# When a unit's copies are issued, and new orders for the first six tiles, in a convolution fused with a two-matmul layer

## Chip, core and metric

One core of one Trainium2 chip runs the whole kernel. The metric is the device time of one execution in microseconds (us); the time of a kernel is the median of its runs.

## What is computed

```python
def _attn_ref(x, weight):                 # x: 8 x 4096 x 192, weight: 8 heads x 7 taps
    w = weight - np.max(weight, axis=-1, keepdims=True)
    w = np.exp(w)
    w = w / (np.sum(w, axis=-1, keepdims=True) + 1e-09)
    ...
    x_unf = x_pad[:, idx, :].reshape(B, S, K, H, group)      # causal: a position and the six before it
    out = np.einsum('hk,bskhg->bshg', w, x_unf)

def _moe_ref(x, w_in, w_out):             # w_in: 192 x 2048, w_out: 2048 x 192
    h = x @ w_in
    g = h * np.cos(h)
    return (g @ w_out).astype(np.float32)
```

The output of the first function, as 32768 rows of 192, is the input of the second. The inputs and the output are float32; the kernel multiplies in bfloat16.

## The kernel before

**Tiles and units.** The 32768 rows are worked in 64 tiles of 512 rows; two tiles make a unit of 1024 rows. A tile t belongs to the unit u = t // 2; an even tile is the first of its unit, an odd one the second.

**A tile.** TensorE (PE) makes eight products h0 to h7 with w_in (`mm1`, L524; six matmuls each) into a ring of three PSUM buffers. For each, ScalarE (ACT) takes the cosine as a shifted sine (s0 to s7, L531) and VectorE (DVE) multiplies it with h to g (L535). The second matmul (`mm2_step`, L573) adds up g times w_out in 64 steps per tile, two matmuls each. It runs behind the first: steps of one tile are spread over the orders of that tile and the next. Its first 32 steps and its last 32 write the same banks with other row halves, so between them the code sets a marker on SP's queue (`Turn`, L203): SP passes it when step 32 is done, and PE waits for it before step 33. The place is called q in the orders. The end of a tile's 64 steps is p; then ACT and DVE copy the result out (P, Q, L592), and O stores it (L595).

**The convolution.** The input of a unit is loaded (L), cast to bfloat16 by GpSimd (POOL) (K, L218), and part of it goes through matmuls with a band matrix on PE (c1, c2: L284, eight matmuls each, with another of the markers on SP's queue between c1 and c2) and ACT's copies (ec1, ec2) into `ct_buf`; SP transposes that by DMA into `ro` (X and x, L326). The other part is transposed raw (T, L353) and its seven taps are multiplied and added up on ACT (a0 to a2, L377) and POOL (R, L386; S, L393 to L396, the last of which writes `ro`). At last SP issues four copies from `ro` into `cT`, the matmuls' input for that unit (U, `spread_raw`, L408 and L409). `cT` has two buffers.

The first three units (0 to 2) go another way: their convolution is done on PE alone (`conv_first`, `conv_rest` r, `conv_part` d1, c1, d2, c2; L236, L486), ACT or DVE copies it out (er, ed, ec, L493, L246; with a small e on ACT, with a capital E on DVE), POOL doubles it (D) and mends its edges (Y), SP transposes it into cT (X, L334).

**What sets the order.** Nothing is scheduled by a planner: the program is written out in strings, one for PE with SP's and POOL's work in it, one for ACT and DVE. `PE_ORDER` and `ACT_ORDER` hold the even and the odd tile of the steady part, `PE_FIRST` and `ACT_FIRST` the first tiles, whose last two entries for ACT are `ACT_ORDER`. "m7" is seven steps of the second matmul, "h3" a product of the first, "w5" five matmuls on zeros into a bank that nobody reads (`keep_warm`, L143), and a letter with "+2" means that work for the unit u + 2. Each engine runs its own instructions in the order in which the strings name them, and waits where data is missing. SP's instructions (all loads, stores, transposes, copies and the markers) form one queue.

**The start.** `LOADS` orders the loads on SP: b is the second half of unit 0, l, r and e are the halves and edge rows of unit 1, and 0 to 3 are quarters of w_out, each by two DMAs (L128); those behind the bar are issued when the first convolution is copied out (L459). POOL casts each quarter (W0 to W3, L124). Step k of the first 32 in tile 0 needs quarter k // 8.

Of the kernel before, what the change touches and what calls it, by code (L numbers as in the profile page):

```python
# [16 lines left out]
def kernel(  # L17
# [9 lines left out]
    B, S, D = x.shape  # L27
    H, K = weight.shape
# [3 lines left out]
    T = 512  # L32
    NT = NTOK // T
    NB = T // 128
    U = 1024
    NU = NTOK // U
    UB = U // 128
# [5 lines left out]
    R = G // NC  # L43
# [9 lines left out]
    PA = 3  # L53
# [66 lines left out]
    wo_src = moe_w_out.rearrange("(i j p) d -> p j i d", i=2, p=128)  # L120

    def cast_wo(q):
        have.add(("wo", q))
        nc.gpsimd.tensor_copy(out=wo[:, q * QP : (q + 1) * QP], in_=wo_f[:, q * QP : (q + 1) * QP])  # L124

# [11 lines left out]
    zero = consts.tile([128, T], BF16)  # L137
# [74 lines left out]
    bf, xk = {}, {}  # L212

    def cast_unit(u, n0=0, n1=UB + 1, copy=nc.gpsimd.tensor_copy):
        if u >= FIRST_RAW:
            xk[u] = xk_pool.tile([128, NC * (UB + 1), 64], BF16, name="xk")
            for n0, n1 in ((NPB, UB + 1), (0, NPB)):
                copy(out=xk[u][:, NC * n0 : NC * n1].rearrange("p (k n) m -> p k n m", k=NC),  # L218
                     in_=x_tiles[u][:, n0:n1].rearrange("p n (m k) -> p k n m", k=NC))
            if u % UPS == 0:  # L220
                nc.gpsimd.memset(xk[u][0 : 128 - OP, 0 : NC * NPB : NPB], 0.0)
            return
        if n0 == 0:
            bf[u] = xb0 if u == 0 else xbf_pool.tile([128, UB + 1, D], BF16, name="x_bf")
        o = 1 if u == 0 else 0
        copy(out=bf[u][:, n0 + o : n1 + o, :].rearrange("p n (h k r) -> p (n h) k r", k=NC, r=R),  # L226
             in_=x_tiles[u][:, n0:n1, :].rearrange("p n (h r k) -> p (n h) k r", k=NC, r=R))

    ct_tiles = {}
    have = {("whole", 0, 0)}  # L230
# [24 lines left out]
    def conv_part(u, c, banks, whole=False):  # L255


        ps = banks()
        nb = UB + 1
        for i in range(4):  # L260
            conv_mm(u, c, ps, i, slice(0, 128), 0, nb, start=i % 2 == 0, stop=i % 2 == 1)
        if u == 1 and c == 0:
            spread_taps(ps[1][:, nb * 2 * G : nb * 2 * G + K])
        yield
        yield
        if u not in ct_tiles:
            ct_tiles[u] = ct_pool.tile([128, UB + 1, NC, 2, 64], BF16, name="ct")
        for b in range(2):
            conv_out(u, c, ps, 0, 0, nb, copies[by[0]], banks=(b,))
            if b and u == 1 and c == 0:  # L270
                nc.scalar.copy(tap, ps[1][:, nb * 2 * G : nb * 2 * G + K])
            if b:
                have.add(("conv", u, c))
            yield

    def conv_unit(u, banks):


        ps = banks()
        sides = [slice(0, 64), slice(64, 128)]  # L280

        def mm(h, side):
            first, last = h % 4 == 0 and h // 4 == side, h % 4 == 3 and h // 4 != side
            return nc.tensor.matmul(  # L284
                out=ps[h // 4][:, 0 : NPB * 4 * G].rearrange("p (m i r) -> p i m r", m=NC * NPB, i=4)[:, h % 4],
                lhsT=band[sides[side], h, 128 - OP : 256 - OP], rhs=xk[u][sides[side], 0 : NC * NPB, R * h : R * (h + 1)],
                start=first, stop=last, skip_group_check=True)

        for h in range(4):
            ms = mm(h, 0), mm(h + 4, 1)  # L290
        turn = Turn()
        turn.mark(*ms)
        yield
        for h in range(4):
            ms = mm(h + 4, 0), mm(h, 1)
            if h == 0:
                turn.wait(*ms)
        yield
        both = ps[0].tensor, ps[0].offset, [ps[0].ap[0][0], OP]
        for n0, n1 in ((1, NPB), (0, 1)):  # L300
            to = ct_bufs[u % 2][0:OP, 2 * NC * min(n0, 1) : 2 * NC * (min(n0, 1) + 1)]
            to = to.rearrange("p (k n) (b w) -> p b k n w", k=NC, b=2)[:, :, :, 0 : n1 - n0]
            nc.scalar.copy(to, bass.AP(both[0], both[1] + 4 * R * n0, [both[2], [T, 2], [NPB * 4 * R, NC], [4 * R, n1 - n0], [1, 4 * R]]))  # L303
            if n0 == 0:
                have.update((("conv", u, 0), ("conv", u, 1)))
            yield
# [32 lines left out]
    tap = consts.tile([128, K], FP32)  # L339
# [42 lines left out]
    def tap_raw(u):  # L382

        p = raw_prod
        for j in range(NG):
            nc.gpsimd.tensor_scalar(out=p[:, j], in0=tap_window(u, PA + j), scalar1=tap[:, PA + j : PA + j + 1],  # L386
                                    scalar2=1.0, op0=ALU.mult, op1=ALU.mult)

    def sum_raw(u):

        assert {("tap", u, j, PARTS[k].start) for j in range(PA) for k in "lr"} <= have
        a, p, add = pa.pop(u), raw_prod, nc.gpsimd.tensor_tensor
        add(out=p[:, 0:PA], in0=p[:, 0:PA], in1=a, op=ALU.add)  # L393
        add(out=p[:, 0:2], in0=p[:, 0:2], in1=p[:, 2:4], op=ALU.add)  # L394
        have.add(("summed", u))
        add(out=stage_of(u)[:, :, NLO * OP : LO], in0=p[:, 0].rearrange("p (k w) t -> p k (w t)", k=NC),  # L396
            in1=p[:, 1].rearrange("p (k w) t -> p k (w t)", k=NC), op=ALU.add)
# [28 lines left out]
    summed = nc.vector.tensor_reduce(out=diag, in_=prod, axis=mybir.AxisListType.X, op=ALU.add)  # L426

    tc.add_manual_dep(nc.sync.nop().ins, summed.ins.name, sync_dep, reason="order of the transfers")
    LOADS = "b l r e | 0 1 2 3"
    for k in LOADS.split("|")[0].split():  # L430
        loads[k]()

    three = {"D": nc.vector.tensor_copy, "A": nc.scalar.copy, "P": nc.gpsimd.tensor_copy}
    for i, k in enumerate("DPDPDPDPDPDPDPAA"):
        q, rows = divmod(i, 4)
# [11 lines left out]
    def conv_first():  # L447

        banks = o_banks()
        for half in range(2):  # L450
            for h in range(H):
                for prev in range(2):
                    nc.tensor.matmul(
                        out=banks[half][:, 0 : 2 * D].rearrange("p (n k h r) -> p h n k r", n=2, k=NC, h=H)[:, h],
                        lhsT=band[:, h, 128 * prev : 128 * prev + 128],
                        rhs=bf[0][:, 2 * half + 1 - prev : 2 * half + 3 - prev, h * G : (h + 1) * G].rearrange(
                            "p n (k r) -> p n k r", k=NC),
                        start=(h == 0 and prev == 0), stop=(h == H - 1 and prev == 1), skip_group_check=True)
            m = copies[half](out=ct_tiles[0][:, 2 * half : 2 * half + 2].rearrange("p n k t w -> p (n k) t w"),  # L459
                             in_=banks[half][:, 0 : 2 * D].rearrange("p (m t w) -> p m t w", t=1, w=64).to_broadcast(  # L460
                                 [128, 2 * NC, 2, 64]))
        tc.add_manual_dep(nc.sync.nop().ins, m.ins.name, sync_dep, reason="order of the transfers")
        for k in LOADS.split("|")[1].split():
            loads[k]()

    def turn_first(half):
        for n in range(2):
# [130 lines left out]
    def finish(t):  # L598
        o_sb[t] = opool.tile([128, NB, D], FP32, name="o_sb")
        for si in range(2):  # L600
            for b in range(2):
# [5 lines left out]

    PE_ORDER = ['m11 h0 m3 h1 S+1 m6 h2 m8 q X+1 h3 K+3 m6 h4 m17 h5 x+1 m9 O p h6 h7 m4', 'm11 h0 m5 h1 R+2 m7 h2 m5 q U+1 h3 m8 h4 m6 c1 m12 c2 T+3 h5 m6 O p L+4 h6 h7 m4']  # L610
    ACT_ORDER = ['s0 s1 s2 a0l2 s3 s4 Q a1l4 a1r4 V s5 s6 s7', 'a0r0 s0 s1 s2 s3 a2l3 s4 a2r4 ec1 Q ec2 s5 P s6 s7']

    PE_FIRST = ["K1 k1 h0a h0b W0 W1 h1 h2 h3 r h4 w5 d11 w4 h5 d21 W2 W3 c11 X0 m1 h6 m11 h7 L2 c21 D1",
# [5 lines left out]
    ACT_FIRST = ["s0a s0b s1 s2 er er s3 s4 ed11 ed21 s5 ec11 s6 ec21 s7",  # L619
                "s0 s1 s2 s3 s4 s5 ec12 ec22 Q P s6 ed12 s7 ed22",  # L620
                "s0 s1 s2 s3 Q s4 P s5 s6 s7",
                "s0 s1 s2 s3 s4 ec1 ec2 Q s5 P s6 s7"] + ACT_ORDER

# [9 lines left out]
    for t in range(NT + 1):  # L633
# [34 lines left out]

        def of_unit(k, v):
            if (k, v) == ("K", 1):  # L670
                cast_unit(1, 0, NB)
            elif (k, v) == ("k", 1):
                cast_unit(1, NB)
            elif k == "Z":
                nc.gpsimd.memset(ct_bufs[v][0:OP, 0 : 2 * NC], 0.0)
            elif (k, v) == ("X", 0):
                turn_unit(0, NB, UB)
# [8 lines left out]
        for k in pe.split():  # L686
# [13 lines left out]
                made = step // (2 * STEPS) - 1  # L700
            elif k == "q":
                assert step % (2 * STEPS) == STEPS
            elif k[0] == "W":
                cast_wo(int(k[1]))
            elif k == "O":
# [43 lines left out]
```

## Time and profile before

| what | before |
|---|---|
| median of 3 runs | 702.14 us (702.13 to 702.61) |
| the profiled execution's own time | 702.85 us |
| its span | 700.9 us |
| PE busy | 693.0 us, 99% |
| DVE busy | 651.1 us, 93% |
| ACT busy | 643.4 us, 92% |
| POOL busy | 577.3 us, 82% |
| PE, matmuls of `mm1` (L524) | 405.5 us, 3078 matmuls |
| PE, matmuls of `mm2_step` (L573) | 413.3 us, 8128 matmuls |
| PE, matmuls on zeros (L143) | 7.7 us, 21 in one bank, and 3 more |
| instruction blocks over DMA (q8) | 92 packets, 1.51 MB |

The matmuls of L524 and L573 use half of PE's rows each and run two at a time, so the busy time of their groups overlaps and sums to more than the span. Idle time of another engine costs only where PE waits for it in the end.

### The profile page before, as it was taken

The page shows a single profiled execution, that of the slowest core. Times are in us where ns is not written, and L with a number is a line of the kernel's source. Part 1 is how long each engine was busy: PE and PEld are TensorE (multiplying, and loading weights), DVE is VectorE, ACT ScalarE, POOL GpSimd, SP SyncE. Part 2 cuts the span into 40 slices and gives each one's busy share as a digit, 9 for nine tenths or more (in the row PEclk, how much of TensorE's full clock was granted, in tenths as well). Part 3 has the DMA queues.
Part 4 walks back from the last instruction along what each step waited for, and adds up shares of the span by engine and source line. Part 5 has one row for each costly group of instructions (what it writes and reads, how often), then busy time and mean ns, then how long its engine had stood idle before and what let it go on. Part 6 is the DMA issues. An engine that isn't in the chain of part 4 may idle for free.

```text
span 700.9 us, 26910 instructions
## 1 busy us (share of the span) xinstructions
PE 693.0 (99%) x11838; PEld 505.5 (72%) x11838; DVE 651.1 (93%) x628; ACT 643.4 (92%) x799; POOL 577.3 (82%) x309
## 2 busy tenths in 40 slices
PE   8999999999999999999999999999999999999998
PEld 4677777777776777777777767777777777777776
DVE  6899999999999999999999999999999999999996
ACT  7889999999999999999999999999999999999875
POOL 6698888899888898888898888988888988887600
PEclk9999999999999999999999999999999999999999
DMA  8992666546765457665556654577654466653232
GB/s 211 204 212 70 147 147 142 106 138 148 169 144 124 115 129 170 152 152 94 146 137 169 146 134 110 128 162 162 149 125 117 126 169 161 146 105 84 68 92 69
DMA packets 163133, 95.99 MB, mean 137 GB/s; under 512 B 68808, under 2 KB 162632, under 8 KB 163016
## 3 DMA queue, kind: packets, MB, share of 16 engines
q1 hardware_dynamic: 162304, 93.30, 57.5%
q8 instruction: 92, 1.51, 0.9%
q0 software_dynamic: 416, 0.79, 0.8%
q14 instruction: 25, 0.20, 0.1%
q10 hardware_dynamic: 296, 0.20, 0.1%
HBM read 31.36 MB, written 25.17 MB: 81 GB/s over the span
## 4 chain that ended last, share of the span: by engine, by line
PE 94%; SPq 2%; DVE 1%; ACT 1%; issue 0%; POOL 0%; POOLq 0%
PE h L524 46%; PE o_ps L573 46%; PE h L284 1%; SPq L409 1%; SPq L408 1%; DVE g L535 1%; ACT cs L531 1%; PE h L573 0%; DVE band L436 0%; ACT ct L493 0%; POOL mask L166 0%; PE h L236 0%; ACT mask L171 0%; ACT ct L459 0%; DVE diag L426 0%
## 5 line engine op out<-in xcount | busy, mean ns | idle before, releaser
L535 DVE TENSOR_TENSOR g<-h,cs 128x1024 bf16<-128x1024 f32 (+1 forms) x513 | 597.3, 1217 | 20.7 <-ACT cs L531 12.2
L531 ACT ACTIVATE cs<-h 128x1024 bf16<-128x1024 f32 (+1 forms) x513 | 510.6, 1022 | 45.0 <-PE h L524 37.3
L573 PEld LDWEIGHTS <-g 64*128 64x128 bf16 x8192 | 353.5, 94 | 102.0 <-issue 0.4
L573 PE MATMUL o_ps<-wo,g 64*128 64x192 bf16 x8128 | 413.3, 243 | 0.0
L524 PE MATMUL h<-cT,w 64*128 64x512 bf16 (+1 forms) x3078 | 405.5, 376 | 1.0 <-DVE g L535 0.6
L393 POOL TENSOR_TENSOR raw_prod<-raw_prod,pa 128x3105 f32<-128x3105 f32 x29 | 164.7, 5679 | 64.4 <-ACT pa L377 64.4
L524 PEld LDWEIGHTS <-w 64*128 64x128 bf16 x3078 | 142.9, 94 | 77.6 <-issue 2.4
L386 POOL TENSOR_SCALAR raw_prod<-rT,tap 128x1035 f32<-128x1035 bf16 x116 | 130.5, 1150 | 0.6 <-DMA rT<-xk 0.5
L377 ACT ACTIVATE pa<-rT,tap 128x575 f32<-128x575 bf16 (+1 forms) x168 | 119.0, 728 | 0.0
L394 POOL TENSOR_TENSOR raw_prod<-raw_prod 128x2070 f32<-128x2070 f32 x29 | 111.6, 3847 | 2.3
L218 POOL CAST xk<-x_f 128x1152 bf16<-128x1152 f32 (+1 forms) x58 | 77.8, 1374 | 1.6 <-DMA x_f<-in_x_dram 1.6
L396 POOL TENSOR_TENSOR ro<-raw_prod 128x1035 bf16<-128x1035 f32 x29 | 69.1, 2381 | 2.3
L592 DVE COPY o_sb<-o_ps 128x384 f32<-128x384 f32 x92 | 48.5, 554 | 19.9 <-PE o_ps L573 19.8
L303 ACT CAST ct_buf<-h 112x384 bf16<-112x384 f32 (+1 forms) x58 | 20.2, 401 | 2.0 <-PE h L284 2.0
L284 PE MATMUL h<-xk,band 64*128 64x72 bf16 x464 | 17.1, 194 | 1.8 <-SPq L203 1.8
L592 ACT COPY o_sb<-o_ps 128x384 f32<-128x384 f32 x34 | 16.0, 474 | 0.1
L284 PEld LDWEIGHTS <-band 64*128 64x128 bf16 x464 | 13.8, 95 | 3.0 <-SPq L203 2.9
L226 POOL CAST x_bf<-x_f 128x768 bf16<-128x768 f32 (+2 forms) x4 | 6.4, 1626 | 6.1 <-DMA x_f<-in_x_dram 6.1
L143 PE MATMUL o_ps<-zero 128*128 128x512 bf16 x21 | 7.7, 519 | 1.3 <-DVE zero L138 1.3
L143 PEld LDWEIGHTS <-zero 128*128 128x128 bf16 x24 | 2.4, 117 | 4.5 <-issue 2.6
L124 POOL CAST wo<-g 128x768 bf16<-128x768 f32 x4 | 3.3, 827 | 2.2 <-DMA g<-in_moe_w_out_dram 2.1
L246 ACT CAST ct<-h 128x432 bf16<-128x432 f32 x8 | 4.0, 536 | 0.0
(67 smaller groups left out, 50.1 us busy)
## 6 DMA issues: line engine op xcount, KB each, us to landing
out_dram<-o_sb SPq DMA_DIRECT2D x63, 384.0 KB, 3.2
x_f<-in_x_dram SPq DMA_DIRECT2D x62, 384.0 KB, 5.1
cT<-ro SPq DMA_DIRECT2D x58, 213.4 KB, 3.4
cT<-ro SPq DMA_DIRECT2D x58, 170.6 KB, 4.4
x_f<-in_x_dram SPq DMA_DIRECT2D x31, 96.0 KB, 3.8
g<-in_moe_w_out_dram SPq DMA_DIRECT2D x8, 192.0 KB, 6.0
ro<-ct_buf SPq DMA_TRANSPOSE x58, 2.4
w<-in_moe_w_in_dram POOLq DMA_DIRECT2D x2, 384.0 KB, 6.2
```

The lines of the kernel that those rows point to most:

```text
L218: copy(out=xk[u][:, NC * n0 : NC * n1].rearrange("p (k n) m -> p k n m", k=NC), in_=x_tiles[u][:, n0:n1].rearrange("p n (m k) -> p k n m", ...
L284: return nc.tensor.matmul(out=ps[h // 4][:, 0 : NPB * 4 * G].rearrange("p (m i r) -> p i m r", m=NC * NPB, i=4)[:, h % 4], lhsT=band[sides ...
L377: nc.scalar.mul(room_of(u)[:, j, part], tap_window(u, j)[:, part], tap[:, j : j + 1])
L386: nc.gpsimd.tensor_scalar(out=p[:, j], in0=tap_window(u, PA + j), scalar1=tap[:, PA + j : PA + j + 1], scalar2=1.0, op0=ALU.mult, op1=ALU. ...
L393: add(out=p[:, 0:PA], in0=p[:, 0:PA], in1=a, op=ALU.add)
L394: add(out=p[:, 0:2], in0=p[:, 0:2], in1=p[:, 2:4], op=ALU.add)
L396: add(out=stage_of(u)[:, :, NLO * OP : LO], in0=p[:, 0].rearrange("p (k w) t -> p k (w t)", k=NC), in1=p[:, 1].rearrange("p (k w) t -> p k ...
L524: nc.tensor.matmul(out=h[:, i, n0 * 128 : n1 * 128], lhsT=w[rows, k, j, :], rhs=rhs, start=(k == 0), stop=(k == NC - 1))
L531: nc.scalar.activation(out=cs[:, :, part], in_=h[:, :, part], func=AF.Sin, bias=math.pi / 2.0, scale=1.0)
L535: nc.vector.tensor_tensor(out=g_tiles[t][:, 2 * j : 2 * j + 2, part], in0=h[:, :, part], in1=cs[:, :, part], op=ALU.mult)
L573: ms.append(nc.tensor.matmul(out=o_ps[tt, b, si], lhsT=g_tiles[tt][rows, f, s * 128 : (s + 1) * 128], rhs=wo[rows, f // 2, f % 2, :], star ...
L592: (copy or copies[b])(o_sb[t][:, 2 * b : 2 * b + 2, :].rearrange("p s d -> p (s d)"), o_ps.pop((t, b)))
```

## The change

The four copies of a unit into cT (U+1) are issued at the head of the odd tile, behind h0, where they stood behind q. The orders of the first six tiles are new: the nine matmuls on zeros in tile 0 (w5, w4) are gone, steps of the second matmul and the other work stand at other places, the first piece of unit 0's second half is copied out by DVE (Er), and quarters of w_out are loaded in the order 1 2 0 3 and cast in the order 0 1 3 2, with quarter 1 ahead of the bar. Assertions are added that the program's order is a legal one; they run while the program is built.

```diff
-    LOADS = "b l r e | 0 1 2 3"
+    LOADS = "b l e r 1 | 2 0 3"
+    def load(k):
+        have.add(("in", k))
+        loads[k]()
...
-    PE_ORDER = ['m11 h0 m3 h1 S+1 m6 h2 m8 q X+1 h3 K+3 m6 h4 m17 h5 x+1 m9 O p h6 h7 m4', 'm11 h0 m5 h1 R+2 m7 h2 m5 q U+1 h3 m8 h4 m6 c1 m12 c2 T+3 h5 m6 O p L+4 h6 h7 m4']
+    PE_ORDER = ['m11 h0 m3 h1 S+1 m6 h2 m8 q X+1 h3 K+3 m6 h4 m17 h5 x+1 m9 O p h6 h7 m4', 'm11 h0 U+1 m5 h1 R+2 m7 h2 m5 q h3 m8 h4 m6 c1 m12 c2 T+3 h5 m6 O p L+4 h6 h7 m4']
...
-    PE_FIRST = ["K1 k1 h0a h0b W0 W1 h1 h2 h3 r h4 w5 d11 w4 h5 d21 W2 W3 c11 X0 m1 h6 m11 h7 L2 c21 D1",
-                "m6 K2 h0 m1 L3 h1 K3 Z1 Z0 m13 q h2 m3 h3 m9 h4 m6 h5 m3 X1 T3 c12 m11 p c22 h6 d12 h7 L4 m17 m4 m1 d22 Y1 D2 m1",
-                "h0 m2 R3 h1 m7 q B3 K4 h2 m11 h3 X2 L5 O m8 h4 Y2 m13 p h5 h6 m9 h7 m7",
-                "h0 S3 m8 h1 m8 q h2 m7 h3 m7 O m1 h4 m3 c1 m4 c2 m6 h5 m4 p T4 h6 h7 m4",
-                "m12 h0 m4 h1 K+3 m5 h2 m7 q h3 m6 h4 m17 h5 X+1 x+1 m9 p h6 h7 O m4",
-                "m11 h0 m4 h1 R+2 m6 h2 m7 q h3 m5 h4 U+1 m7 c1 m8 c2 m3 h5 T+3 L+4 m9 p O h6 h7 m4"]
-    ACT_FIRST = ["s0a s0b s1 s2 er er s3 s4 ed11 ed21 s5 ec11 s6 ec21 s7",
-                "s0 s1 s2 s3 s4 s5 ec12 ec22 Q P s6 ed12 s7 ed22",
+    PE_FIRST = ["K1 k1 h0a h0b W0 W1 h1 h2 W3 h3 r h4 d11 h5 c11 d21 W2 m1 h6 m7 X0 m4 h7 L2 c21 D1 m1",
+                "m7 K2 L3 h0 K3 h1 Z1 Z0 m12 q h2 m3 h3 m9 h4 m6 h5 m3 X1 c22 T3 c12 m11 p d12 h6 h7 L4 m21 d22 Y1 D2 m1 R3 m1",
+                "h0 m2 h1 m7 q B3 h2 m8 K4 h3 X2 m10 h4 m1 Y2 m13 p h5 h6 L5 O m9 h7 m10",
+                "h0 m1 S3 m7 h1 m5 q h2 m7 h3 m10 O h4 m1 c1 m4 c2 m5 h5 m5 p T4 h6 h7 m10",
+                "m6 h0 m4 h1 K+3 m5 h2 m7 q h3 m6 h4 m17 h5 x+1 O m9 p X+1 h6 h7 m4",
+                "m11 R+2 h0 m7 U+1 h1 m3 h2 m7 q h3 m5 h4 m8 c1 m7 c2 m4 T+3 h5 L+4 m8 p O h6 h7 m4"]
+    ACT_FIRST = ["s0a s0b s1 s2 Er er s3 s4 ed11 ed21 s5 ec11 s6 ec21 s7",
+                "s0 s1 s2 s3 s4 s5 ec12 ec22 P Q s6 ed12 s7 ed22",
                 "s0 s1 s2 s3 Q s4 P s5 s6 s7",
                 "s0 s1 s2 s3 s4 ec1 ec2 Q s5 P s6 s7"] + ACT_ORDER
```

More of the change, by code (lines that the diff above doesn't have):

```diff
@@ L122, in cast_wo @@
     def cast_wo(q):
+        assert ("in", str(q)) in have
         have.add(("wo", q))
@@ L224, in cast_unit @@
             bf[u] = xb0 if u == 0 else xbf_pool.tile([128, UB + 1, D], BF16, name="x_bf")
+        if n1 > UB:
+            have.add(("cast", u))
         o = 1 if u == 0 else 0
@@ L255, in conv_part @@
     def conv_part(u, c, banks, whole=False):
+        assert ("cast", u) in have
         ps = banks()
@@ L298, in conv_unit @@
         yield
+        assert ("zero", u % 2) in have
         both = ps[0].tensor, ps[0].offset, [ps[0].ap[0][0], OP]
@@ L384, in tap_raw @@
         p = raw_prod
+        have.add(("product", u))
         for j in range(NG):
@@ L389, in sum_raw @@
     def sum_raw(u):
-        assert {("tap", u, j, PARTS[k].start) for j in range(PA) for k in "lr"} <= have
+        assert {("product", u)} | {("tap", u, j, PARTS[k].start) for j in range(PA) for k in "lr"} <= have
         a, p, add = pa.pop(u), raw_prod, nc.gpsimd.tensor_tensor
@@ L428 @@
     tc.add_manual_dep(nc.sync.nop().ins, summed.ins.name, sync_dep, reason="order of the transfers")
-    LOADS = "b l r e | 0 1 2 3"
+    LOADS = "b l e r 1 | 2 0 3"
+    def load(k):
+        have.add(("in", k))
+        loads[k]()
     for k in LOADS.split("|")[0].split():
-        loads[k]()
+        load(k)
     three = {"D": nc.vector.tensor_copy, "A": nc.scalar.copy, "P": nc.gpsimd.tensor_copy}
@@ L463, in conv_first @@
         for k in LOADS.split("|")[1].split():
-            loads[k]()
+            load(k)
     def turn_first(half):
@@ L670, in of_unit @@
             if (k, v) == ("K", 1):
+                assert ("in", "l") in have
                 cast_unit(1, 0, NB)
             elif (k, v) == ("k", 1):
+                assert {("in", "r"), ("in", "e")} <= have and 1 in bf
                 cast_unit(1, NB)
             elif k == "Z":
+                have.add(("zero", v))
                 nc.gpsimd.memset(ct_bufs[v][0:OP, 0 : 2 * NC], 0.0)
@@ L702 @@
                 assert step % (2 * STEPS) == STEPS
+            elif k[0] == "I":
+                load(k[1])
             elif k[0] == "W":
```

## The prediction

> **What bounds the kernel now.** I read the page first (span, busy time), then the list of waits, then the chain of waits in order of time, and last the timeline at the places that these name. The page:
>
> ```profile
> span 700.9 us, 26910 instructions
> PE 693.0 (99%) x11838; PEld 505.5 (72%) x11838; DVE 651.1 (93%) x628; ACT 643.4 (92%) x799; POOL 577.3 (82%) x309
> ```
>
> TensorE (PE) is busy 99% of the span, so only its 7.9 us without work, and work of its own that computes nothing, can be won. The list of waits has just one entry for PE that can recur in the steady part, at the convolution's matmuls (L284), and its releaser is a marker on SP's queue (L203):
>
> ```profile
> PEld L284 <- SPq L203: 2.9, 5, 0.8
> PE h L284 <- SPq L203: 1.8, 4, 0.6
> ```
>
> The chain of waits in order of time (start, length, what) shows what these cost. The twelve matmuls at which h6 and h7 stand together end each tile and so recur once per unit (two tiles):
>
> ```profile
> 190.79 1.29 PE h L524 x12
> 211.97 1.30 PE h L524 x12
> 233.91 1.29 PE h L524 x12
> 255.59 1.29 PE h L524 x12
> ...
> 361.48 1.30 PE h L524 x12
> 382.66 1.30 PE h L524 x12
> 404.54 1.29 PE h L524 x12
> 426.23 1.29 PE h L524 x12
> ```
>
> A unit takes 21.18 us (190.79 to 211.97; 361.48 to 382.66). Four units take longer: 21.94, 21.68, 21.88 and 21.69. The excess is 0.76 + 0.50 + 0.70 + 0.51 = 2.47 us. The timeline at the first of them:
>
> ```profile
> 218.09 0.62 SPq L408 DMA_DIRECT2D cT<-ro  x1
> 218.76 1.79 SPq L409 DMA_DIRECT2D cT<-ro  x1
> ...
> 221.25 0.63 SPq L409 DMA_DIRECT2D cT<-ro  x1
> 222.00 0.30 PE L284 MATMUL h<-xk,band 64*128 64x72 bf16 x8 [0.58 <-SPq L203]
> ```
>
> SP issues the four copies of a unit into cT in a row, from 218.09 to 221.88. One issue takes 1.79 instead of 0.62. Behind them on SP's queue stands the marker that releases the second eight of the L284 matmuls, and PE waits for it. Not the landing of the copies is late but the queue behind their issue.
>
> **The change part by part: the copies.** U+1 moves in the odd tile's order from behind the marker q to behind h0. On SP's queue this moves all four issues past one marker, that of q; nothing else of SP's is passed. A unit without the stall, in the timeline:
>
> ```profile
> 101.65 2.68 SPq L326 DMA_TRANSPOSE ro<-ct_buf  x2
> 104.44 0.51 SPq L595 DMA_DIRECT2D out_dram<-o_sb  x1
> 104.45 2.38 POOL L396 TENSOR_TENSOR ro<-raw_prod 128x1035 bf16<-128x1035 f32 x1
> ...
> 112.19 0.63 SPq L408 DMA_DIRECT2D cT<-ro  x1
> ...
> 114.17 0.67 SPq L409 DMA_DIRECT2D cT<-ro  x1
> ...
> 115.36 0.29 PE L284 MATMUL h<-xk,band 64*128 64x72 bf16 x8
> ```
>
> The copies need the transposes into ro (issued by 104.33) and the sum on POOL, done at 106.83. In the old order they wait on for q until 112.19, take until 114.84, and leave 0.5 us before PE wants the next marker at 115.36. So any issue that is 1.2 us slow stalls PE. In the new order they start at 106.83, end at 109.5 (four issues, 2.65 us) or 110.7 with one slow issue, and the q marker, now behind them, is wanted at about 112.1: 2.6 or 1.4 us to spare. The c marker at 115.36 then has SP idle ahead of it. What is late next is nothing on PE: rT's transpose, the store and the x load behind the c marker start at most 0.6 us sooner. The copies' bytes now run beside POOL's and PE's work of 107 to 112; the buffer that they fill was last read a tile earlier. I price that move at nothing, its cover being those 1.4 us, and the gain at the whole 2.47 us. Bounds: 2.47 gained at the upper end; nothing gained where the slow issue comes back elsewhere.
>
> **The first six tiles.** Steps of the second matmul done at the end of tiles 0 to 5 were 12, 87, 144, 196, 260, 324 and become 13, 87, 147, 202, 260, 324. From the end of tile 4 both kernels stand at the same place with the same real work done, so the six orders are worth what PE idles, or spends on zeros, up to there. Rows of the start:
>
> ```profile
> 8.88 0.96 DVE L459 CAST ct<-o_ps 128x768 bf16<-128x768 f32 x1 [1.02 <-PE o_ps L453]
> ...
> 9.86 5.48 SPq L128 DMA_DIRECT2D g<-in_moe_w_out_dram  x8
> ...
> 13.30 2.41 DVE L535 TENSOR_TENSOR g<-h,cs 128x1024 bf16<-128x1024 f32 x2 [0.18 <-ACT cs L531]
> ...
> 14.53 1.50 ACT L493 CAST ct<-o_ps 128x768 bf16<-128x768 f32 x2
> ...
> 15.52 1.25 PE L143 MATMUL o_ps<-zero 128*128 128x512 bf16 x5
> ...
> 16.53 1.68 POOL L124 CAST wo<-g 128x768 bf16<-128x768 f32 x2
> ...
> 16.99 2.36 DVE L535 TENSOR_TENSOR g<-h,cs 128x1024 bf16<-128x1024 f32 x2 [1.27 <-ACT cs L531]
> 17.06 1.02 PE L143 MATMUL o_ps<-zero 128*128 128x512 bf16 x4
> ...
> 18.27 0.82 PE L524 MATMUL h<-cT,w 64*128 64x512 bf16 x6 [0.19 <-DVE g L535]
> ...
> 19.50 0.26 PE L573 MATMUL o_ps<-wo,g 64*128 64x192 bf16 x2
> ...
> 20.05 0.83 POOL L124 CAST wo<-g 128x768 bf16<-128x768 f32 x1 [1.85 <-DMA g<-in_moe_w_out_dram]
> ...
> 21.46 0.82 PE L524 MATMUL h<-cT,w 64*128 64x512 bf16 x6
> ...
> 22.11 0.67 PE L573 MATMUL o_ps<-wo,g 64*128 64x192 bf16 x12
> 22.60 0.83 PE L524 MATMUL h<-cT,w 64*128 64x512 bf16 x6
> ```
>
> *The nine matmuls on zeros* (15.52 and 17.06) fill time in which PE waits for DVE: h5 starts at 18.27, released by g3, not by the zeros. Removing them is worth nothing by itself.
>
> *Er.* The second half of unit 0's convolution is copied out by ACT in two pieces (1.50 us), ahead of the sine of tile 0's h3; DVE idles 1.27 us for that. Now DVE copies the first piece, behind its product at 13.30, that is from 15.71. The trace has no such copy on DVE with this shape; the nearest row is L459, 0.96 us with as many written elements, the other bound ACT's 0.75. I take 0.96: the product g3 can start at 16.69 instead of 16.99, and ACT's sine is ready before (one piece of 0.75 less). So g3, h5, its sine, g5 and with them h7 move 0.3 us: h7 from 21.46 to about 21.15. Bounds 0 to 0.5.
>
> *Loads and casts of wo.* The order of the quarters was 0 1 2 3 and is 1 | 2 0 3; the first now goes ahead of the wait for the first convolution, and the edge rows ahead of x's second half. The casts on POOL go W0, W1, W3, W2. So quarter 0, which the first step needs, now lands in third place. In the old order quarters 0 and 1 were there when POOL came (16.53, no wait), the third place at 20.05 (1.85 us of waiting). If the third place still lands at 20.05, W0 ends at 20.88 where PE wants it at about 19.2 (h5 at 17.95, then 0.65 for it and 0.5 for a convolution part; old first step: 19.50): 1.4 to 1.7 us of PE standing, of which the 0.3 of Er is lost too. What held the third place in the old order is, I think, one block of 16 KB of instructions that entered the DMA engines just ahead:
>
> ```profile
> q1 hardware_dynamic: 937, 0.63, 108.0%
> q8 instruction: 1, 0.02, 3.5%
> ```
>
> That is the DMA view of 16.5 to 18.5 (queue, packets, MB, share). The eight loads lie on q1, 0.197 MB each (128 x 2 x 192 floats), and in that window q1 moves 0.63 MB in 2 us, so a place of two loads takes about 1.25 us: third place would be some 1.25 us behind second, that is before 18.6 (second place was there by 17.36, when its cast began without a wait). The block comes at a count of PE instructions, and PE now has 18 instructions fewer in front (nine zeros and their weight loads), so it comes after more real work, by my count after h5 (g3 from 16.69 by 1.22, h5 at 17.95), when quarter 0 is through. Then W0 is cast by 18.9 to 19.4, W1 0.83 later, and PE is not held. By the Trainium skill, "Runtime: NRT & Kernel Launch", section "Instruction fetch mechanics", a block is 256 instructions and the cost of crossing into one is mostly hidden; by that rule alone nothing would be lost at either place. The trace agrees on the size (the row above) and not on the cost, if the 1.85 us is the block's.
>
> *Sum of the start.* Tile 1's h0 begins at 22.60 with 18 steps done, and six steps take 0.49 us (22.11 to 22.60), so 20 steps would stand at 22.76. The new order has 20 steps ahead of h0: h7 from 21.15 to 21.8 (0.65), eight steps 0.65: 22.4. Gain 0.36 us; with W0 late, a loss of 1.1.
>
> *The rest of tiles 1 to 5.* The steps move between orders, the convolution's parts of unit 2 swap, P and Q swap, and K, L, O, R, S, X shift by a few steps. O and X only shift within the same stretch between two of SP's markers, so SP issues them as before. PE runs full behind 22.60 already (busy time in a window: PE, its weight loads, DVE, ACT, POOL, then granted clock):
>
> ```profile
> 22.60:50.00 27.40, 27.40 (x451) 19.76 (x448) 24.34 (x23) 22.95 (x27) 22.06 (x20) 1.00 1.09 227
> ```
>
> So nothing is to be won there; a wait may arise where DVE (24.34 of 27.40, with the least room) falls behind. I take 0, bounds -0.2 to +0.5. The asserts add no instruction. In all: 2.47 + 0.36 = 2.83 us.
>
> The profiled execution took 702.85 us (span 700.9 and 1.95 around it), 0.71 over the median of 702.14. The sum makes it 700.0 for such an execution and 702.14 - 2.83 = 699.3 for the median.
>
> **The rivals.**
> (1) *Quarter 0 late.* As above: the copies' gain stays, the start loses 1.1: 702.14 - 2.47 + 1.1 = 700.8. For it: the third place at 20.05. Against: the block's place.
> (2) *The slow issue moves.* If a transpose and a copy are both hit, SP reaches q late and PE waits there: gain of the copies lost, 702.14 - 0.36 = 701.8, or half of it, 700.6. Against: 1.4 us to spare with one hit, and two hits must fall within 5 us.
> (3) *A cold clock.* Without the zeros PE has idle stretches between h4 and h7. What a cold PE costs is in the first zeros:
>
> ```profile
> 3.21 3.96 PE L143 MATMUL o_ps<-zero 128*128 128x512 bf16 x9
> ```
>
> 0.44 us each against 0.25 at 15.52. They last until 7.17, from a first one before 3.21, so some 4 to 6 us at near half speed, 2 to 3 us lost: 699.3 + 2.5 = 701.8. By the Trainium skill, "TensorE: Matmul & The Clock Gate", Part 1, the clock falls after an idle window of about 3.4 us; by that rule it would not fall here, as the longest stretch I count is 1.7 us (h5's neighbours to a late W0), and no run here shows the limit.
> (4) *Slower: the copies block q.* SP now waits for POOL's sum with q's marker behind it, and PE's second half of 32 steps behind that. It decides as soon as the sum ends later than 109.4 (112.1 less 2.65), that is 2.6 us later than in the row at 104.45. Each microsecond beyond costs 29 us over the 29 units; 0.2 us would make 702.14 + 5.8 - 2.8 = 705. For it: POOL is 82% busy and its sums wait for ACT. Against: none of its inputs is moved in the steady orders.
>
> **How the numbers follow.** Forecast 0.60 (698.7 to 700.3), rival 1 0.20, rival 2 0.10, rival 3 0.05, rival 4 0.05. A measurement of this kernel tells about 0.2%, 1.4 us, from no change: faster means below 700.74. Faster: 0.60, half of rival 1, a third of rival 2, and no more: 0.73. Slower (above 703.5): rival 4 and a part of 3, with what I do not see in the orders: 0.08. Same: 0.19. The range is 698.7 to 701.4: it leaves out rivals 3 and 4 and the upper half of rival 2.
>
> **What would show it.** Right: units of 21.18 us throughout, no wait of PE for L203, the copies' issues at about 107, 5 us ahead of q; slow issues still there but without a wait behind them; W0 cast before 19.5; tile 1's h0 near 22.4; no zeros at 15 to 18. Wrong: W0 at 20 or later and PE idle ahead of its first step (rival 1); granted clock under 1.00 before 30 us (rival 3); PE waiting for SP at the matmuls of L573 in the odd tile (rivals 2 and 4).

## The result, and the profile after

| | before | after |
|---|---|---|
| median (22 runs each, side by side) | 702.10 us (701.06 to 702.85) | 700.24 us (699.79 to 703.22) |
| ratio of the times | | 0.9982, 95% interval 0.9975 to 0.9989 |
| profiled execution, its own time | 702.85 us | 700.14 us |
| its span | 700.9 us | 698.1 us |

The forecast for the median was 699.3 us with a range of 698.7 to 701.4. The change is faster by 1.9 us, less than the 2.83 us of the sum. The two profiled executions differ by 2.7 us, almost the sum; where the median lost the rest is the subject of the experiments.

The page of after, its first line and its line of busy time (share of the span, number of instructions):

```profile
span 698.1 us, 26890 instructions
PE 689.2 (99%) x11828; PEld 524.7 (75%) x11829; DVE 651.7 (93%) x629; ACT 642.3 (92%) x798; POOL 577.5 (83%) x309
```

The list of PE's waits in after (total us, times, longest). The code has moved by some lines: the second matmul is L583, the first L534, the late convolution c1 and c2 L288, SP's marker L204, the U copies L414 and L415, the casts of w_out L125.

```profile
PE o_ps L144 <- DVE zero L139: 1.3, 1, 1.3
PE h L239 <- POOL x_bf L229: 1.1, 1, 1.1
PE h L534 <- DVE g L545: 1.0, 2, 0.6
PE o_ps L583 <- POOL wo L125: 0.9, 1, 0.9
PE o_ps L463 <- ACT x_bf L229: 0.4, 1, 0.4
PE o_ps L463 <- DVE band L446: 0.3, 1, 0.3
PE o_ps L463 <- POOL band L446: 0.2, 1, 0.2
PE h L534 <- DVE cT L488: 0.2, 1, 0.2
```

The entry that carried the prediction, PE's convolution waiting for SP's marker, is gone. Every entry left belongs to the start, and one is new: the first step of the second matmul waits 0.9 us for a cast of w_out. The chain of waits at the same units as before:

```profile
190.64 1.29 PE h L534 x12
211.82 1.29 PE h L534 x12
233.00 1.29 PE h L534 x12
254.18 1.30 PE h L534 x12
...
381.26 1.29 PE h L534 x12
402.44 1.29 PE h L534 x12
423.62 1.29 PE h L534 x12
```

Every unit takes 21.18 us, the four formerly long ones too. The timeline shows how the copies now stand, first a usual unit, then one with a slow issue:

```profile
104.30 2.38 POOL L402 TENSOR_TENSOR ro<-raw_prod 128x1035 bf16<-128x1035 f32 x1
...
106.71 0.63 SPq L414 DMA_DIRECT2D cT<-ro  x1
...
108.69 0.68 SPq L415 DMA_DIRECT2D cT<-ro  x1
```

```profile
446.91 1.97 SPq L414 DMA_DIRECT2D cT<-ro  x1
448.92 0.62 SPq L415 DMA_DIRECT2D cT<-ro  x1
```

The sum on POOL ends at 106.68, the copies run from 106.71 to 109.37, where the prediction had 106.83 to 109.5. The slow issue still occurs (1.97 us), but the last copy of its unit ends at 449.54, 1.6 us before PE goes on behind the marker q at 451.15; 1.4 us had been reckoned for this case.

The start, in the timeline of after:

```profile
15.60 0.95 DVE L503 CAST ct<-o_ps 128x768 bf16<-128x768 f32 x1
...
16.59 2.36 DVE L545 TENSOR_TENSOR g<-h,cs 128x1024 bf16<-128x1024 f32 x2
...
16.68 0.53 PE L239 MATMUL h<-x_bf,band 128*128 128x216 bf16 x4 [1.12 <-POOL x_bf L229]
...
17.88 0.82 PE L534 MATMUL h<-cT,w 64*128 64x512 bf16 x6 [0.64 <-DVE g L545]
...
19.20 3.14 POOL L125 CAST wo<-g 128x768 bf16<-128x768 f32 x4 [2.57 <-DMA g<-in_moe_w_out_dram]
...
20.07 0.26 PE L583 MATMUL o_ps<-wo,g 64*128 64x192 bf16 x2 [0.90 <-POOL wo L125]
```

```profile
22.69 0.51 PE L583 MATMUL o_ps<-wo,g 64*128 64x192 bf16 x8
23.02 1.26 PE L534 MATMUL h<-cT,w 64*128 64x512 bf16 x10
```

The piece that DVE copies takes 0.95 us (0.96 was taken), the product g3 follows at 16.59, h5 at 17.88 (17.95 was forecast, 18.27 before). Up to there all is as reckoned. Then quarter 0 of w_out, third in the order of loads, is there only at 19.20; POOL stands 2.57 us for it and PE 0.90. Tile 1 starts at 23.02, where 22.4 was forecast (the terms given there, 21.15 and twice 0.65, add up to 22.45).

### The profile page after: what moved, and what is told of

It is laid out like the page before. It is cut to its first block, busy times and chain, and to the rows that moved or that the text cites. A ratio compares the mean times of both kernels' runs of the same rounds, so it can differ in the third digit from the quotient of the medians.

```text
span 698.1 us, 26890 instructions
## 1 busy us (share of the span) xinstructions
PE 689.2 (99%) x11828; PEld 524.7 (75%) x11829; DVE 651.7 (93%) x629; ACT 642.3 (92%) x798; POOL 577.5 (83%) x309
## 4 chain that ended last, share of the span: by engine, by line
PE 97%; DMA 2%; POOL 0%; DVE 0%; ACT 0%; issue 0%; SPq 0%; POOLq 0%
PE o_ps L583 48%; PE h L534 47%; PE h L288 1%; DMA x_f<-in_x_dram 1%; DMA g<-in_moe_w_out_dram 1%; PE h L583 0%; POOL mask L167 0%; PE h L239 0%; POOL wo L125 0%; ACT mask L172 0%; DVE diag L432 0%; DVE prod L429 0%; SPq L106 0%; DVE o_sb L612 0%; POOL quarter L149 0%
## 5 line engine op out<-in xcount | busy, mean ns | idle before, releaser
L583 PEld LDWEIGHTS <-g 64*128 64x128 bf16 x8192 | 365.2, 94 | 91.4 <-issue 1.2
L583 PE MATMUL o_ps<-wo,g 64*128 64x192 bf16 x8128 | 418.9, 243 | 0.9 <-POOL wo L125 0.9
L534 PE MATMUL h<-cT,w 64*128 64x512 bf16 (+1 forms) x3078 | 411.2, 376 | 1.2 <-DVE g L545 1.0
L534 PEld LDWEIGHTS <-w 64*128 64x128 bf16 x3078 | 157.0, 94 | 69.2 <-issue 1.3
L288 PE MATMUL h<-xk,band 64*128 64x72 bf16 x464 | 17.9, 194 | 0.0
L288 PEld LDWEIGHTS <-band 64*128 64x128 bf16 x464 | 15.1, 95 | 0.1
L144 PE MATMUL o_ps<-zero 128*128 128x512 bf16 x12 | 4.7, 551 | 1.3 <-DVE zero L139 1.3
L325 POOL COPY ct<-ct 128x1728 bf16<-128x1728 bf16 x2 | 3.3, 1627 | 3.1 <-ACT ct L249 3.1
L125 POOL CAST wo<-g 128x768 bf16<-128x768 f32 x4 | 3.1, 827 | 2.6 <-DMA g<-in_moe_w_out_dram 2.6
```

The lines of the kernel that those rows point to most:

```text
L288: return nc.tensor.matmul(out=ps[h // 4][:, 0 : NPB * 4 * G].rearrange("p (m i r) -> p i m r", m=NC * NPB, i=4)[:, h % 4], lhsT=band[sides ...
L534: nc.tensor.matmul(out=h[:, i, n0 * 128 : n1 * 128], lhsT=w[rows, k, j, :], rhs=rhs, start=(k == 0), stop=(k == NC - 1))
L583: ms.append(nc.tensor.matmul(out=o_ps[tt, b, si], lhsT=g_tiles[tt][rows, f, s * 128 : (s + 1) * 128], rhs=wo[rows, f // 2, f % 2, :], star ...
```

## Experiments

Three theories stood against one another. **A:** without the nine matmuls on zeros the granted clock of PE falls in part of the executions, and that costs the median. **B:** only the arrival of quarter 0 costs something. **C:** the profile of before held more stall than its typical execution, so a median can't gain the whole sum. Later came **D**, on what makes an issue slow. Kernels of one group ran on the same chip and share their runs of before.

### First group: the parts one by one (before here: 702.42 us, 701.07 to 703.18, 17 runs)

**The zeros back, into the gaps of the new order** (in a bank that nothing waits for):

```diff
-... h2 W3 h3 r h4 d11 h5 c11 d21 W2 ...
+... h2 W3 h3 r h4 w4 d11 w3 h5 c11 w4 d21 W2 ...
```

> The changed kernel, with matmuls on zeros put back only into stretches where PE stands anyway: four behind h4, three ahead of h5, four ahead of the first step of the second matmul, in the bank that ACT has copied out. The timed executions of the changed kernel lay at 699.8 to 700.4 in 14 of 22 and at 700.8 to 703.2 in 8, and those 8 show a mean clock of 0.995 to 0.998. Theory A (the clock falls in some executions because PE stands at 15.5 to 20 us): no execution under 0.999, none over 700.7, median 700.1. Theory B (the arrival of quarter 0 of w_out scatters): the scatter stays, up to 703. Either way no more than 0.2 us on the good executions.

Measured: 700.34 us (699.97 to 701.1, 7 runs), ratio 0.997 (0.9959 to 0.9981), all clocks at 1.0. So A holds as far as seven runs go. But the times scatter by 1.1 us at full clock, and the profiled one, the slowest, shows why in its list of waits:

```profile
PE o_ps L583 <- POOL wo L125: 1.0, 1, 1.0
```

Its cast of quarter 0 began at 20.10, against 19.20 above. B is there as well.

**The copies alone:** before with U+1 moved, nothing else.

```diff
-'m11 h0 m5 h1 R+2 m7 h2 m5 q U+1 h3 ...'
+'m11 h0 U+1 m5 h1 R+2 m7 h2 m5 q h3 ...'
...
-"m11 h0 m4 h1 R+2 m6 h2 m7 q h3 m5 h4 U+1 m7 c1 ..."
+"m11 h0 m4 U+1 h1 R+2 m6 h2 m7 q h3 m5 h4 m7 c1 ..."
```

> The kernel before, with the four copies of a unit issued behind the odd tile's h0 (also in tile 5), and nothing else. My steps: the stalls behind the copies' issues go, and the zeros stay, so no execution with a low clock. The profile of before lost 2.47 us to them: 699.6 by that profile. Theory C (that profile was one with more stalls than most: it was 0.7 above the median of before): 2.47 less 0.75, so 700.4. If the slow issues only moved: 702.

Measured: 700.09 us (699.93 to 700.13, 5 runs), ratio 0.9966 (0.9953 to 0.9978). The time lies between the two that were expected, 699.6 and 700.4. The first matmul of a tile stands 0.14 us ahead of before's profile at tile 6 and 2.64 us ahead at the end: 2.50 us from the steady part. Another 0.20 us is won from tile 5 to tile 6, where U+1 was moved too. Before has a short stall there, which the list of waits holds among PE's weight loads (five, against four of its matmuls):

```profile
72.49 0.18 PEld L284 LDWEIGHTS <-band 64*128 64x128 bf16 x8 [0.24 <-SPq L203]
```

Against the median it is 2.33 us. This part alone is worth more than the whole change was against its own runs of before (1.86 us), and the scatter falls from 2.1 us to 0.2.

**The first tiles alone:** after with U+1 back behind q.

```diff
-'m11 h0 U+1 m5 h1 R+2 m7 h2 m5 q h3 ...'
+'m11 h0 m5 h1 R+2 m7 h2 m5 q U+1 h3 ...'
...
-"m11 R+2 h0 m7 U+1 h1 m3 h2 m7 q h3 m5 h4 m8 c1 ..."
+"m11 R+2 h0 m7 h1 m3 h2 m7 q h3 m5 h4 U+1 m8 c1 ..."
```

> The changed kernel with the four copies back behind q, in the steady order and in tile 5. My steps: the new orders alone give 0.2 to 0.4 us, 701.8. Theory A: besides that, executions 0.6 to 3 us slower with a clock of 0.995 to 0.998 in about a third, so a median about that of before, 702.0, and some at 704 to 705. Theory B: a third as slow, but with the clock at 1.0.

Measured: 701.75 us (700.83 to 703.32, 11 runs), ratio 0.9995 (0.9986 to 1.0004). Six of the eleven have a mean clock of 0.995 to 0.998; none is as long as the 704 to 705 us expected for some. Its profile caught one. Busy time of PE by windows; behind it the granted clock, then DMA share and GB/s:

```profile
11.03:14.45 3.42, 3.08 (x38) 1.00 1.11 310
14.45:17.86 3.41, 1.67 (x21) 1.00 1.11 327
17.87:21.28 3.41, 3.32 (x18) 0.50 1.21 209
21.28:24.69 3.41, 3.41 (x58) 1.00 1.06 305
```

From 17.87 to 21.28, 3.41 us, the granted clock is 0.50: that is A seen directly. In the window just before PE was busy 1.67 of 3.41 us, with no pause longer than 1.10 us. By the Trainium skill, "TensorE: Matmul & The Clock Gate", Part 1, the clock is set by a free-running window of 3.41 us. The trace agrees on that length. The Trainium skill has the clock fall after an idle window there; here a half busy one was enough.

The list of waits of the same profile has the old stall again:

```profile
PE h L288 <- SPq L204: 1.4, 2, 0.8
```

**Quarter 0 first:** after with another order of loads and casts.

```diff
-    LOADS = "b l e r 1 | 2 0 3"
+    LOADS = "b l e r 0 | 1 2 3"
...
-    PE_FIRST = ["K1 k1 h0a h0b W0 W1 h1 h2 W3 h3 r h4 d11 h5 c11 d21 W2 m1 ...
+    PE_FIRST = ["K1 k1 h0a h0b W0 W1 h1 h2 W2 h3 r h4 d11 h5 c11 d21 W3 m1 ...
```

> The changed kernel with the quarters of w_out loaded 0 | 1 2 3 and cast 0 1 2 3, so that the quarter needed first lands first; all else as changed. In the changed kernel's profile PE waits 0.9 us for quarter 0's cast. Rival 1 of the prediction: this wait goes, h0 of tile 1 comes at 22.2 to 22.4 in place of 23.02, 699.5 in good executions. Theory A: the stretch in which PE stands is 0.9 us shorter, so fewer executions with a low clock, but some. Theory B: no scatter at all. If quarter 2 or 3 is late in its place: gain under 0.5.

Measured: 699.51 us (699.41 to 699.82, 5 runs), ratio 0.9958 (0.9946 to 0.9971). The timeline:

```profile
16.59 1.72 POOL L125 CAST wo<-g 128x768 bf16<-128x768 f32 x2
...
19.19 0.26 PE L583 MATMUL o_ps<-wo,g 64*128 64x192 bf16 x2
...
22.46 0.83 PE L534 MATMUL h<-cT,w 64*128 64x512 bf16 x6
```

PE no longer waits for a cast, and tile 1 starts at 22.46: the 22.4 of the prediction. So B holds: the late quarter had cost the profile of after the 0.56 us from 22.46 to 23.02. Behind tile 1 more is won than was reckoned. Counting the steps already done, this version is 0.30 us ahead of before's profile at tile 1 and 0.72 at tile 6. Of the 0.4 between, 0.2 come in tile 3, for a cause that no run isolates, and 0.2 in tile 5, as with the copies alone.

### Second group: zeros and quarter 0 together (before here: 701.86 us, 700.98 to 703.17, 29 runs)

**Both:** quarter 0 first as above, and `w4` behind h4, `w3` ahead of h5.

```diff
-... h2 W3 h3 r h4 d11 h5 c11 d21 W2 ...
+... h2 W2 h3 r h4 w4 d11 w3 h5 c11 d21 W3 ...
```

> The changed kernel with quarter 0 of w_out loaded and cast first and with the matmuls on zeros back in the gaps of the first tile. Theory A (the granted clock falls for 3.4 us in part of the executions because the first tile now has idle matmul stretches): no execution below clock 0.999, and the time of the version with quarter 0 first, 699.5 (699.3 to 699.8). Theory B (what the changed start lost is the arrival of quarter 0 alone): also 699.5, so this run does not separate A from B; it tells whether the zeros are worth anything once quarter 0 is early. If the zeros delayed needed work, by up to 0.3 us: 699.8.

Measured: 699.59 us (699.57 to 699.67, 5 runs), ratio 0.9966 (0.9954 to 0.9978), no clock below 0.999. In the window that held 1.67 us of work with the first tiles alone, PE is now busy nearly throughout:

```profile
14.45:17.86 3.41, 3.28 (x30) 1.00 1.11 328
```

The zeros delay nothing: tile 1 starts at 22.45.

**Quarter 0 last:** the opposite dose. Only the loads change; the casts keep their order, so all four wait for quarter 0.

```diff
-    LOADS = "b l e r 1 | 2 0 3"
+    LOADS = "b l e r 1 | 2 3 0"
```

> The changed kernel with quarter 0 of w_out loaded and cast last. Theory A: a longer idle stretch of the matmuls in the first tile, so the clock falls (0.995 to 0.998) in more than a third of the executions, at 701.5 to 704; theory B: only the wait for quarter 0 grows, W0 done about 21.5 instead of 20.0, tile 1 starts about 1.5 us later, 701.3 to 702, with the clock at 0.999 or above in every execution.

Measured: 702.99 us (701.11 to 704.96, 12 runs), ratio 1.001 (0.9999 to 1.0022). Five executions at 0.999 or above lie at 701.11 to 701.46, where B had 701.3 to 702; seven lie at 702.99 to 704.96 with clocks of 0.995 to 0.998. Both theories hold side by side. The profile, one at full clock:

```profile
20.38 3.14 POOL L125 CAST wo<-g 128x768 bf16<-128x768 f32 x4 [3.87 <-DMA g<-in_moe_w_out_dram]
21.26 0.26 PE L583 MATMUL o_ps<-wo,g 64*128 64x192 bf16 x2 [2.13 <-POOL wo L125]
```

**After again**, unchanged.

> The changed kernel again, as the yardstick on the same chip. Theory A: about a third of its executions with a clock of 0.995 to 0.998, each 0.7 to 3 us above the others; the rest at 699.8 to 700.4. Theory B: one group without low clocks.

Measured: 701.17 us (700.04 to 702.79, 11 runs), ratio 0.9992 (0.9982 to 1.0001). Four of eleven have a clock of 0.995 to 0.997, at 701.88 to 702.79. The other seven fall into two groups, 700.04 to 700.29 and 700.96 to 701.21. The profile, at 701.17, is of the second group: quarter 0 cast at 20.28, PE waiting 1.8 us for it. On this chip the change as it stands was worth hardly anything.

**Before again**, unchanged.

> The kernel before again, for a second profile of it. Theory C (the profiled execution of before lay 0.75 us above the median because its stalls behind the slow U copies were longer than in a typical execution): the stalls of this profile add up to less than 2.47 us, and its time is lower by as much. Rival: the stalls again add up to 2.4 to 2.5 us whatever its time, and the difference sits in the start.

Measured: 701.61 us (701.4 to 702.22, 8 runs), ratio 0.9997 (0.9987 to 1.0006). Its profile took 701.79 us, 1.06 less than the first one of before. The wait behind SP's marker:

```profile
PE h L284 <- SPq L203: 0.7, 2, 0.3
```

0.7 us in two waits, where the first profile has 1.8 in four. By the starts of the tiles its start is 0.15 us later, and from tile 7 to the end it wins 1.18 us: its stalls cost 2.47 - 1.18 = 1.29 us. C holds for these two profiles.

### Third group: what makes an issue slow (before here: 702.56 us, 701.52 to 703.53, 17 runs)

Laid beside the blocks of TensorE's instructions (queue q8, 16 KB each), the U copies of before show a pattern: all five issues of over 1.0 us overlap a block, and the longest of the 101 that overlap none is 0.72 us. Ten others overlap a block as well and take 0.60 to 0.95 us, so not every meeting makes a slow issue. To test this as a cause, the blocks were moved: 12 matmuls on zeros ahead of the first tile were cut into 64 narrow ones.

```diff
-    keep_warm(3)
+    keep_warm(16, cols=96)
...
-    keep_warm(9)
+    keep_warm(48, cols=96)
```

> The kernel before with the 12 matmuls on zeros ahead of the first tile cut into 64 narrow ones (96 columns instead of 512): the same columns, 52 more matmuls and 52 more weight loads. Theory D (a U copy's issue is slow because a 16 KB block of TensorE's instructions, one for each 256 of them, is fetched during it): 104 instructions are 104 / 736 of a unit's 21.18 us, so each block comes 3.0 us earlier against the work; the meeting drifts 1.02 us later per unit, so the slow issues and the stalls move to the units three further on: from those at 218.8, 241, 389.4, 412, 559.8 to those at about 282, 304, 452, 474 and 622, 644, with a first pair at about 113 and 134. No slow issue at 218 to 242; each slow issue overlaps a block. Time about that of before, 700.9 to 703.2, somewhat more if a fourth pair stalls. Rival (the slow issue comes from the other transfers in flight at that point of the unit): they stay at 218.8, 241, 389.4, 412.

Measured: 701.94 us (701.27 to 703.02, 10 runs), ratio 0.9997 (0.9988 to 1.0007). The timeline of SP's queue where before had its first slow issue, and where D puts one:

```profile
218.94 0.62 SPq L408 DMA_DIRECT2D cT<-ro  x1
219.60 0.60 SPq L409 DMA_DIRECT2D cT<-ro  x1
220.25 0.61 SPq L408 DMA_DIRECT2D cT<-ro  x1
220.91 0.62 SPq L409 DMA_DIRECT2D cT<-ro  x1
```

```profile
135.51 1.08 SPq L408 DMA_DIRECT2D cT<-ro  x1
136.64 0.62 SPq L409 DMA_DIRECT2D cT<-ro  x1
```

And the DMA view of 134.9 to 136.6 (queue, packets, MB, share):

```profile
q1 hardware_dynamic: 163, 0.19, 58.6%
q8 instruction: 1, 0.02, 4.6%
```

No U copy between 218 and 242 is slow any more. The ones of over 0.9 us start at 135.5, 283.1, 305.0, 474.4 and 644.6, three units on, each beside a block; D had 134, 282, 304, 474 and 644. At about 113, 452 and 622, where D had one too, a block overlaps the first of the copies and none is slow. The blocks set the places where an issue can be slow. How slow an issue gets varies (1.23 at most here, 1.79 in before), and in this profile none was slow enough to make PE wait.

**Quarter 0 first, again.**

> The version with quarter 0 of w_out loaded and cast first, again, as the best one: 699.4 to 699.8 with no clock under 0.999 by theory A, since nothing but the two waits of 1.1 and 0.6 us is left in the first tile; if these alone make the clock fall, executions of 700.2 to 702.5 at 0.995 to 0.998 as well.

Measured: 699.65 us (699.5 to 701.37, 7 runs), ratio 0.9967 (0.9957 to 0.9978). Four at 699.5 to 699.65, three at 700.63 to 701.37 with a clock of 0.997. Two waits ahead of h5, 1.15 and 0.61 us in this profile, and one of 0.15 are all that is left between 14 and 23 us: the clock still drops now and then.

### Fourth group: the zeros by themselves (before here: 701.48 us, 700.89 to 702.66, 15 runs)

**Both, again:**

> The changed kernel with quarter 0 first and with the zeros back in the gaps, again. Theory A (the clock falls only where the zeros are gone): every execution at 0.999 or above and 699.5 to 700.0. Rival (the clock falls now and then whatever the zeros do; the 5 executions so far were luck, where 3 of 12 of the version without zeros fell): about a quarter of the executions at 0.995 to 0.998 and 700.2 to 702.5.

Measured: 699.38 us (699.31 to 699.55, 5 runs), ratio 0.9964 (0.9952 to 0.9977), all clocks at 0.999 or above.

**Before with nothing but the zeros taken out:**

```diff
-... h3 r h4 w5 d11 w4 h5 d21 W2 W3 ...
+... h3 r h4 d11 h5 d21 W2 W3 ...
```

> The kernel before with nothing changed but w5 and w4 taken out of the first tile's order. The prediction held these zeros worth nothing by themselves: then the times are those of before, 700.9 to 703.2, and no clock is under 0.999. Theory A: a part of the executions, between a tenth and a half, shows a clock of 0.995 to 0.998 and is 0.7 to 3 us longer, up to 706; the median 0 to 0.7 above that of before.

Measured: 701.65 us (700.4 to 702.6, 11 runs), ratio 1.0 (0.9991 to 1.0009). Seven of eleven have a clock of 0.998, at 701.38 to 702.6; the four at full clock lie at 700.4 to 701.52. No timed execution of before beside these groups, 78 in all, is under 0.999. So A is shown by this one edit. That the median did not rise all the same has a reason in the steady part: the profile, at full clock, takes 2.2 us less than the first one of before from tile 7 to the end. With 18 instructions fewer ahead the blocks lie elsewhere, and the slowest U copy takes 1.28 us, which fits D; one profile does not show how far that goes for the other executions.

Put together: in kernels without zeros in tile 0 (after, after again, first tiles alone, quarter 0 first twice, quarter 0 last, before without zeros) 35 of 79 executions have a clock of 0.998 or less. In the changed kernels with zeros (back in the gaps, and both, twice) it is none of 17.

## Why the prediction was right, point by point

- **The copies: right in mechanism, and in size but for one stall.** 2.47 us was reckoned; the starts of the tiles give 2.50 from tile 6 on, in after and in the copies alone. The copies' issue from 106.71 to 109.37, the slow issues that stay harmless, and the units of 21.18 us came as written. The sum over four units left out the stall in tile 5, worth another 0.20. Rivals 2 and 4 did not happen: no wait of PE for SP's marker is left, in any kernel that has the copies moved.
- **Er: right.** 0.95 against 0.96 us, h5 at 17.88 against 17.95.
- **Quarter 0: wrong (rival 1, given 0.20).** The step that failed is "the block comes after h5, when quarter 0 is through". It came at 16.42, ahead of h5, and the third place was cast at 19.20, where 18.9 to 19.4 was forecast for the end of W0, which came at 20.02. Against 22.46 with quarter 0 first, tile 1 lost 0.56 us in the profile of after and 1.6 in that of after again (24.10), where the prediction had 1.4 to 1.7 us of standing.
- **Why the third place is late: likely a block, as the prediction thought.** In all thirteen profiles that show when the quarter in third place is cast, whichever it is, the cast begins at 19.2 to 20.3. In before the loads of w_out land about 0.6 us apart, except that 2.11 us lie between the fourth and the fifth (17.26 and 19.37), with the block of 17.01 to 18.12 in that stretch. With the first block moved to 12.39 (the narrow zeros) that step is gone (18.36, 18.96, 19.49, 20.07), but the first load lands 1.1 us later than in before, at 16.56 against 15.45, and the third place is cast at 19.61 all the same. So the block seems to delay whatever loads are still to land. This is one run, and it was not made for this question.
- **The rest of tiles 1 to 5: mis-sized.** "I take 0" turned out as 0.4 us won, 0.2 in tile 3 and 0.2 in tile 5, inside the bounds given. In after the late quarter and this gain nearly cancel: 0.17 us ahead at tile 7, where the start had been reckoned at 0.36. That the profiled execution took 700.14 with 700.0 forecast is luck in this part.
- **The zeros: wrong (rival 3, given 0.05).** "Removing them is worth nothing by itself" left out the clock. I compared the longest pause, 1.7 us, with the idle window of about 3.4 us of the Trainium skill, "TensorE: Matmul & The Clock Gate", Part 1, and found it too short. The runs show that a window half filled with pauses can be enough: the clock fell behind one with 1.67 us busy of 3.41, and in 12 of the 33 executions of the changed kernel. In the first 22 these are 0.7 to 3 us longer (700.83 to 702.01 at 0.997 and 0.998, and 702.91 to 703.22 at 0.995, against a median of 700.17 at full clock). One window of 3.41 us at half speed takes 0.0024 off the mean clock of 698 us, so by this estimate 0.997 and 0.998 stand for one such window and 0.995 for two. Rival 3's 2.5 us lies between the prices of one, 0.7 to 1.8, and of two, 2.7 to 3.1.
- **From the profile to the median: wrong.** For the median the sum for the profiled execution was taken from 702.14. But that profile, 0.71 us above the median, held more of the very stall that the change removes: before again had 1.29 us of it. A gain of 2.47 was there for that execution, not for every one. After the change the full-clock executions of the first 22 have a median of 700.17, just where the profile lies. This makes some 0.7 of the 0.94 us by which the median missed the forecast. The profiled execution's own miss, 0.14, and the low clocks, 0.07 (700.24 against 700.17), are most of the rest.
- The forecast range held the time because it was drawn to take in a late quarter 0; the error from the profile to the median, larger than any other, happened to stay within the range as well.

## What to carry to other kernels

A stall that depends on where instruction blocks fall differs from execution to execution: take its size from several profiles, and move the exposed work away from the deadline rather than hoping for another phase. Matmuls on zeros in a gap are not idle work to be cleared away: count how busy TensorE is in each stretch of 3.4 us, wherever it begins, not only its longest pause, and leave them in where a stretch would drop to about half. When loads are reordered, the first one needed goes first: here that and the zeros give 699.3 to 699.7 us in all ten executions. The order of loads alone is as quick at full clock, but three of its twelve executions were 1 to 2 us longer at a lower clock.

## What the runs showed of the hardware

- **One block of instructions slows the issue of other transfers.** A 16 KB block of TensorE's instructions (92 in 700 us) stretches an SP issue of 0.62 us that it meets to as much as 2.28 us (in the copies alone). In all fourteen profiles, no copy that meets no block takes more than 0.80 us. By the Trainium skill, "Runtime: NRT & Kernel Launch", section "Instruction fetch mechanics", a block is 256 instructions and crossing into one costs little, mostly hidden. The size agrees: before's 23676 matmuls and weight loads make 92 blocks, 257 for each, and 52 matmuls and 52 weight loads more moved the slow issues by three units. TensorE itself did not stand for a block in the lists of waits; the cost fell on SP's queue.
- **The clock can fall on half a window.** A window of 3.41 us with PE busy 1.67 us was followed by one at 0.50. In the profiles of the kernels that have shown low clocks, the least busy stretch of this length in the first tile, wherever it begins, holds 1.28 to 1.65 us of work; in those with zeros there 2.4 or more, and none of these fell.
- **The windows run free of the kernel.** The traces' record of full clock begins at 4.63 to 7.93 us in the fourteen profiles, and each later change of the clock in a trace comes a whole number of windows behind that (692.91 us, or 203 windows of 3.413, in eleven of them). So the windows lie over the pauses now one way, now another. The profile of after has almost the same pauses ahead of h5 as the one that fell (1.12 and 0.64 us against 1.10 and 0.66), but its window begins at 15.71 instead of 14.45, holds a little more work, and the clock stayed up behind it:

```profile
15.71:19.12 3.41, 1.81 (x16) 1.00 1.35 306
19.12:22.54 3.42, 2.52 (x42) 1.00 0.93 228
```

- **Busy time does not draw the line exactly.** After again has two windows in a row of about half, and the one behind them is still at 1.00:

```profile
15.82:19.23 3.41, 1.71 (x16) 1.00 1.54 308
19.23:22.65 3.42, 1.65 (x30) 1.00 0.83 142
22.65:26.06 3.41, 3.41 (x59) 1.00 1.07 309
```

So 1.67 us of work let the clock fall in one execution, and 1.65 did not in another. The limit lies near half a window, as far as these traces tell. That the place of the windows decides which executions fall fits, and is not shown: just one profile caught a fall.
